# Eight sets of second-layer weight forms, at another place in the planner's order

## The chip, the cores and the metric

The kernel runs on one core of a Trainium2 chip. The metric is the device time of one execution in microseconds, as the median of several runs. A profile of one execution stands beside the times. Engines are named as the profile does: PE (TensorE matmul; PEld is its weight load), DVE (VectorE), ACT (ScalarE), POOL (GpSimd) and SP (SyncE, which issues most DMAs).

## The reference

Eight batch elements pass through an attention block and then an MLP-mixer block, all in float32:

```
x / rms(x) * g on q and k                # 12 heads, 448 positions, 64 wide
attn = softmax(q k^T / 8);  x = attn v   # -> x: 448 x 768 for each element
u  = x + (relu(x^T w_tok1) w_tok2)^T     # token mixing, 256 hidden
out = u + relu(u w_ch1) w_ch2            # channel mixing, 1536 hidden
```

## The kernel before, in words

**Elements and phases.** The elements are taken in turn. For element b the kernel emits token mixing (`tok1`, L833, and `tok2`, L876), the first channel layer (`ch1`, L987) and the second one (`plain_2`, L1041, for b = 1; `ch2`, L1055, from b = 2 on). The attention of element b+1 is merged in between as steps (`att_step`, L656; `big_step`, L587): scores into PSUM (L458), exponentials on ACT (L462), sums of them on DVE (L499), values (L531), and for the pair of heads after it the loads of q and k (L1375), squares on ACT (L1394), their sums on DVE (L1408), a Newton root (L1449 to L1451), the scaling (L420) and a transposition (L435). "Product (m, i)" below is `ch1`'s product i of hidden block m, m = 0 to 2, i = 0 to 6.

**Fewer products by sums of weights.** Both channel layers use schemes that trade products for sums of blocks, so that sums of the weights ("forms") have to be made first, on the chip.
- `sum_items` (L242) makes the first layer's: SP loads four blocks into a tile of the pool `raw` (L276), POOL makes four more (L249 to L252), SP stores them to DRAM (L256). `ch1` reads them through `load_units` (L915, DMA L927), up to seven weight units ahead.
- `form_items` (L291) makes the second layer's, in eight sets g = 0 to 7. A set takes three `raw` tiles a, b and c out of a pool of five. `load` issues four DMAs on SP (L304 twice, L305, L306) from the stored plain weights into a and b. Four `part`s then make 16 additions of 128x128 on POOL (L320), the last part also three copies (L324) and, on POOL's own DMA queue, two stores (L310, L311). Only `ch2` of element 2 and after needs them, and `load_units` reads none of them until all eight sets have been emitted.

**`ch1`'s seven products.** Each goes to a PSUM tile `m_ps` of two that alternate, and is drained: i = 0 and 4 by a copy on ACT (L1009, L1021), the others by an addition on DVE (L1005). After i = 4, POOL makes two additions (L1005) into `hb` and `r[2]`; DVE's addition of i = 5 reads that `r[2]`.

**What sets the order.** PE, DVE, ACT and POOL run in the order in which the program emits them. Items carry a cost, `run` (L166) adds the costs up on a planner's clock, and `later(us, fn)` (L158) emits a function when that clock has passed its due time. SP is not in the list of the hand-ordered engines (L88): its DMAs stand in nearly, but not exactly, the order of emission. `form_items` is called behind element 1's token mixing (L1240). Counted from that call, in the planner's units, and added up from the items' costs: product (0,4) is emitted at 29.8, (1,1) at 53.7, (1,2) at 58.8, (1,3) at 63.6, (1,4) at 67.0, (1,5) at 73.5, (2,1) at 88.6, (2,4) at 103.1, (2,5) at 108.4. The twelve halves of `plain_2` begin at 119.2 (the third is at 139.0, the fifth at 160.9, the eighth at 180.5). The second half of element 2's x leaves for DRAM at 187.0 (`send_x`, L780, DMA L786), is loaded back, turned, at 194.0 (`load_x`, L792, DMAs L795 and L798), and element 2's token mixing, which reads it at L837 and L844, begins at 204.2.

Of the kernel before, what the change touches and what calls it, by code (L numbers as in the profile page):

```python
# [83 lines left out]
def whole(ctx, tc, shifted, pre, q, k, v, g_q, g_k, moe_w_tok1, moe_w_tok2, moe_w_ch1, moe_w_ch2, out):  # L84
# [73 lines left out]
    def later(us, fn):  # L158

        at = clock[0] + us  # L160
        i = len(pending)
        while i and pending[i - 1][0] > at:
            i -= 1
        pending.insert(i, (at, fn))
# [37 lines left out]
    def raw_tile():  # L202
        return raw_pool.tile([P, WCOLS, 2], U32, name="raw")
# [87 lines left out]
    def form_items():  # L291


        G, FORMS_FROM, FORMS_EVERY = range(8), 10.0, 20.0
        plain = lambda g: wp2[:].rearrange("p (m h x k t) n -> p x h t m k n", m=3, h=2, x=2, k=3)[
            :, g // 4, g // 2 % 2, g % 2]
        made = ws2[:].rearrange("p (f c) n -> p c f n", c=8)
        eight = lambda t: t[:].rearrange("p n w -> p (n w)").bitcast(F32).rearrange("p (q n) -> p q n", q=8)

        def load(g):  # L300
            a, b, c = st["form", g] = [eight(raw_tile()) for _ in range(3)]
            src = plain(g)
            for m in range(2):
                nc.sync.dma_start(out=a[:, 3 * m:3 * m + 3], in_=src[:, m])  # L304
            nc.sync.dma_start(out=a[:, 6:8], in_=src[:, 2, 0:2])  # L305
            nc.sync.dma_start(out=b[:, 7], in_=src[:, 2, 2])  # L306

        def send(g):
            a, b, c = st.pop(("form", g))
            nc.gpsimd.dma_start(out=made[:, g, 0:8], in_=c)  # L310
            nc.gpsimd.dma_start(out=made[:, g, 8:NF9], in_=b[:, 0:7])  # L311
            st["formed"] += 1

        def part(g, i):
            a, b, c = st["form", g]
            at = dict(d=a[:, 4], s=a[:, 6], v=a[:, 7], y=a[:, 3])
            at.update({(m, k): a[:, 3 * m + k] if 3 * m + k < 8 else b[:, 7] for m in range(3) for k in range(3)})
            at.update({f: c[:, f] if f < 8 else b[:, f - 8] for f in range(NF9)})
            for o, x, op, y in W_STEPS[4 * i:4 * i + 4]:
                nc.gpsimd.tensor_tensor(  # L320
                    out=at[o], in0=at[x], in1=at[y], op=ALU.add if op == "+" else ALU.subtract)
            if i == 3:
                for f, x in W_SINGLE:
                    nc.gpsimd.tensor_copy(out=at[f], in_=at[x])  # L324
                send(g)

        for g in G:
            at = FORMS_FROM + g * FORMS_EVERY
            later(at, lambda g=g: load(g))
            for i in range(4):  # L330
                later(at + 8.0 + 2.5 * i, lambda g=g, i=i: part(g, i))
# [890 lines left out]
    for b in range(B):  # L1222
        early, double = middle_items(b)
        if b == 0:
            early, last = first_items(
                tok1_items(0, 0) + x_items(0, 1) + tok1_items(0, 1) + early, double, some)
        else:
            if b > 1 and in_next(b - 1):

                y, z = sends(b - 1, y_order(b - 1)[:4]), left  # L1230
                left = [y[0], y[1], z[0], y[2], z[1], y[3]]
            run(merge(tok1_items(b, 0), left[:2]))
            begin, early = merge(tok1_items(b, 1) + early[:3 * KC], left[2:]), early[3 * KC:]
            if b == 1 and not shifted:
                run(merge(begin, sums[5:9]))
                early, begin = merge(early[:8], sums[9:]) + early[8:], []
            elif b == 1:
                early, begin = merge(begin + early[:8], sums[5:]) + early[8:], []
            if b == 1:
                form_items()  # L1240
            tail, keep = (4, 2) if b == 1 else (11, 6)
            last, ends = double[-tail - keep:-tail], double[-tail:]
            double = double[:-tail - keep]
            early = begin + early + double
# [33 lines left out]
class Start:  # L1278
# [67 lines left out]
    def plain(self, p):  # L1346

        return p < 2 * self.NPAIR
# [177 lines left out]
```

## Time and profile before

| | us |
|---|---|
| median of 3 runs | 1302.79 (1302.38 to 1304.1) |
| the profiled execution | 1300.44 |
| its span, first to last instruction | 1298.5 |
| mean granted PE clock | 0.993 |
| busy PE / DVE / ACT / POOL | 1250.2 / 793.8 / 392.3 / 383.4 |
| L320, 128 additions: first and last start | 300.5, 408.2 |
| L320, one: least / median / longest | 0.448 / 0.456 / 1.382 |
| L310 and L311, 8 each: one on POOL | 0.905 and 0.971 |
| landing of L310 / L311, median | 5.0 / 6.5 |
| landing of the loads L304 | 4.0 |

Lines of the timeline read: start, duration, engine, line, operation, output<-input, shape, count, and in brackets the idle time of the engine before it with what ended it. The table by windows gives, for each stretch of the span, its length, each engine's busy time with the number of instructions, the granted PE clock, the busy share of the DMA engines and what they moved in GB/s. A line of the waits is: who waited, for whom, us in total, how often, the longest.

### The profile page before, as it was taken

To read this page: it belongs to the slowest core of one execution; us is meant where nothing else is said; L and a number is where in the kernel's file an instruction comes from. 1 tells how busy PE (TensorE), PEld (TensorE's weight loads), DVE (VectorE), ACT (ScalarE), POOL (GpSimd) and SP (SyncE) were. 2 spreads that over 40 slices of the span, in tenths; PEclk is the share of its full clock that TensorE was granted. 3 is DMA by queue.
4 is the path that set the end of the run, shared out by engine and by line. 5 is a ranking of instruction groups with operands and counts; after the bars stand their busy time and mean duration, and the time that the engine had idled before them with its cause. 6 is when DMAs were issued, how large, how long until landed. Compare 5 with 4: busy or idle time off the path is not lost.

```text
span 1298.5 us, 20006 instructions
## 1 busy us (share of the span) xinstructions
PE 1250.2 (96%) x7228; PEld 889.8 (69%) x7228; DVE 793.8 (61%) x1229; ACT 392.3 (30%) x781; POOL 383.4 (30%) x641
## 2 busy tenths in 40 slices
PE   5998999997899999999999999999999999999996
PEld 3444444455654577895787868785887868797996
DVE  6988769754655256765658366765558456554233
ACT  5663433222322043312343034311343033300210
POOL 1303440047887012231132222231122322131231
PEclk9999999998999999999999999999999999999998
DMA  9667585997899567685766867595866964386553
GB/s 207 174 183 180 155 226 146 216 258 208 248 275 217 121 148 172 152 229 117 173 167 144 218 141 175 140 224 116 188 156 149 232 140 136 117 200 156 180 174 79
DMA packets 492864, 228.37 MB, mean 176 GB/s; under 512 B 375508, under 2 KB 453332, under 8 KB 492756
## 3 DMA queue, kind: packets, MB, share of 16 engines
q1 hardware_dynamic: 476178, 213.10, 66.6%
q0 software_dynamic: 3584, 12.06, 3.0%
q10 hardware_dynamic: 12994, 1.84, 0.8%
q8 instruction: 59, 0.97, 0.3%
q14 instruction: 49, 0.40, 0.1%
HBM read 184.26 MB, written 42.66 MB: 175 GB/s over the span
## 4 chain that ended last, share of the span: by engine, by line
PE 84%; DVE 6%; DMA 3%; POOL 2%; issue 2%; ACT 1%; SPq 1%; ACTq 0%; DVEq 0%; POOLq 0%
PE m_ps L999 23%; PE m_ps L1065 21%; PE s_ps L458 9%; PE o_ps L531 9%; PE m_ps L879 5%; PE m_ps L969 5%; PE m_ps L1048 4%; PE t_ps L837 2%; PE m_ps L837 2%; DMA ws<-raw 1%; PE m_ps L511 1%; PE d_ps L511 1%; POOL raw L320 1%; PE t_ps L432 1%; DVE raw L348 1%
## 5 line engine op out<-in xcount | busy, mean ns | idle before, releaser
L1065 PE MATMUL m_ps<-hb,unit 128*128 128x224 f32 x1440 | 277.2, 354 | 0.0
L1065 PEld LDWEIGHTS m_ps<-hb,unit 128*128 128x128 f32 x1440 | 271.0, 190 | 8.8 <-issue 7.7
L999 PE MATMUL m_ps<-tu,unit 128*128 128x224 f32 x1008 | 201.6, 355 | 1.3 <-ACT r L1009 1.3
L999 PEld LDWEIGHTS m_ps<-tu,unit 128*128 128x128 f32 x1008 | 189.1, 190 | 15.0 <-issue 9.9
L462 ACT ACTIVATE e<-s_ps 128x448 f32<-128x448 f32 x294 | 138.3, 549 | 174.6 <-PE s_ps L458 166.2
L999 PE MATMUL m_ps<-uT,unit 128*128 128x224 f32 x756 | 153.6, 358 | 13.7 <-DVE hb L1005 11.5
L999 PEld LDWEIGHTS m_ps<-uT,unit 128*128 128x128 f32 x756 | 144.0, 192 | 21.6 <-DVE hb L1005 13.0
L458 PE MATMUL s_ps<-qkT 64*64 64x448 f32 x1260 | 144.6, 545 | 0.8 <-ACT x L819 0.8
L531 PE MATMUL o_ps<-e,v 64*64 64x448 f32 x1148 | 131.4, 538 | 0.3 <-ACT uT L568 0.2
L1005 DVE TENSOR_TENSOR hb<-m_ps,r 128x448 f32<-128x448 f32 x63 | 39.1, 621 | 120.5 <-POOL r L1005 68.9
L499 DVE TENSOR_TENSOR es<-es,e 128x896 f32<-128x896 f32 x90 | 103.2, 1146 | 14.4 <-ACT e L462 9.0
L1005 POOL TENSOR_TENSOR hb<-r,r 128x448 f32<-128x448 f32 x21 | 23.8, 1135 | 245.4 <-ACT r L1021 245.4
L458 PEld LDWEIGHTS s_ps<-qkT 64*64 64x64 f32 x1260 | 45.7, 132 | 69.6 <-issue 60.1
L531 PEld LDWEIGHTS o_ps<-e,v 64*64 64x64 f32 x1148 | 46.4, 133 | 63.1 <-issue 58.4
L1006 ACT ACTIVATE hb<-hb 128x448 f32<-128x448 f32 x84 | 48.4, 577 | 111.8 <-DVE hb L1005 76.6
L879 PE MATMUL m_ps<-w_sb,h 128*128 128x448 f32 x192 | 75.3, 544 | 3.3 <-DVE uT L884 3.3
L1438 POOL TENSOR_TENSOR nt<-rs 128x56 f32<-128x56 f32 (+1 forms) x57 | 19.5, 341 | 198.1 <-DVE rs L1430 195.1
L1080 POOL TENSOR_TENSOR uT<-uT,r 128x448 f32<-128x448 f32 x42 | 51.4, 1240 | 78.3 <-DVE r L1080 46.6
L320 POOL TENSOR_TENSOR raw<-raw 128x128 f32<-128x128 f32 x128 | 68.0, 551 | 16.1 <-DMA ws<-raw 5.9
L884 DVE TENSOR_TENSOR uT<-uT,m_ps 128x448 f32<-128x448 f32 x48 | 29.3, 613 | 63.0 <-PE m_ps L879 63.0
L1005 DVE TENSOR_TENSOR r<-m_ps,r 128x448 f32<-128x448 f32 x42 | 26.1, 622 | 64.7 <-PE m_ps L999 64.7
L1408 DVE TENSOR_REDUCE ms<-sq 128x28 f32<-128x896 f32 (+2 forms) x44 | 47.4, 1080 | 28.6 <-ACT sq L1394 25.0
(141 smaller groups left out, 1585.0 us busy)
## 6 DMA issues: line engine op xcount, KB each, us to landing
unit<-ws SPq DMA_DIRECT2D x267, 384.0 KB, 4.1
raw<-in_moe_w_ch_dram SPq DMA_DIRECT2D x72, 256.0 KB, 3.5
v<-in_v_dram SPq DMA_DIRECT2D x96, 112.0 KB, 3.9
xs<-xt SPq DMA_DIRECT2D x56, 168.0 KB, 4.4
out_dram<-turned SPq DMA_DIRECT2D x168, 56.0 KB, 2.0
qk_t<-in_q_dram SPq DMA_DIRECT2D x144, 56.0 KB, 3.7
qk_t<-in_k_dram SPq DMA_DIRECT2D x144, 56.0 KB, 3.6
x<-xs SPq DMA_DIRECT2D x42, 192.0 KB, 4.1
```

The lines of the kernel that those rows point to most:

```text
L320: nc.gpsimd.tensor_tensor(out=at[o], in0=at[x], in1=at[y], op=ALU.add if op == "+" else ALU.subtract)
L458: nc.tensor.matmul(out=pss[i][rows_of(i, a), 0:S], lhsT=qkT[h, 1, k * D:(k + 1) * D], rhs=qkT[h, 0, :], start=True, stop=True)
L462: nc.scalar.activation(out=e[:, i, :], in_=pss[i][:, 0:S], func=AF.Exp)
L499: nc.vector.tensor_tensor(out=es[:], in0=(es if k > 1 else st["e", t, 0])[:], in1=st["e", t, k][:], op=ALU.add)
L531: nc.tensor.matmul(out=st["o", p][a * D:(a + 1) * D, 0:S], lhsT=vt[rows, k * D:(k + 1) * D], rhs=e[rows, :], **kw)
L837: nc.tensor.matmul(out=st["t1", h][jc][:, 0:HC], lhsT=w1_sb[:, c, jc * P:(jc + 1) * P], rhs=st["x", b, h][:, :, c, :], start=start and c = ...
L879: nc.tensor.matmul(out=ps[:, 0:S], lhsT=st["h1", jc][:, cc * P:(cc + 1) * P], rhs=w2_sb[:, jc].rearrange("p c r -> p (c r)"), start=(jc == ...
L969: nc.tensor.matmul(out=ps, lhsT=a[:, o + 2 * half, :], rhs=natural(half * KF + t) if wide else u[:, half * KC + t, :], start=(t == 0 and h ...
L999: nc.tensor.matmul(out=ps[:, j * HS:(j + 1) * HS], lhsT=w[:, t, j, :], rhs=m, start=(t == 0), stop=(t == KC - 1))
L1005: add = lambda e, o, x, y: e.tensor_tensor(out=o, in0=x, in1=y, op=ALU.add)
L1048: nc.tensor.matmul(out=ps, lhsT=w[:, t, :], rhs=natural(half * KF + t), start=(half == 0 and t == 0), stop=(half == 1 and t == KF - 1))
L1065: nc.tensor.matmul(out=ps[:, x * HS:(x + 1) * HS], lhsT=st["w"][:, tile_at % 6, :], rhs=hb[:, X_SLOT[f], i, :], start=(i == 0), stop=(i == 3))
```

## The change

Two numbers in `form_items`. Set g was due at 10 + 20 g planner units after the call, its parts 8.0, 10.5, 13.0 and 15.5 later; now it is due at 55 + 18 g. The last part's due time goes from 165.5 to 196.5. Nothing else differs; all sets, operations and DMAs are the same.

```diff
     def form_items():
...
-        G, FORMS_FROM, FORMS_EVERY = range(8), 10.0, 20.0
+        G, FORMS_FROM, FORMS_EVERY = range(8), 55.0, 18.0
...
         for g in G:
             at = FORMS_FROM + g * FORMS_EVERY
             later(at, lambda g=g: load(g))
             for i in range(4):
                 later(at + 8.0 + 2.5 * i, lambda g=g, i=i: part(g, i))
```

## The prediction, on record

> **What bounds the kernel now.** I began with the table by windows, because the page has PE busy for 96% of the span: only the stretches where it is not can give anything.
>
> ```profile
> 276.00:320.00 44.00, 34.94 (x221) 24.54 (x220) 25.11 (x45) 12.47 (x27) 25.22 (x49) 0.88 0.79 225
> 320.00:360.00 40.00, 34.08 (x230) 24.35 (x228) 23.29 (x32) 14.03 (x30) 34.51 (x63) 1.00 0.89 250
> 360.00:400.00 40.00, 40.00 (x224) 22.36 (x224) 25.58 (x41) 13.90 (x29) 36.01 (x64) 1.00 1.02 254
> 400.00:437.00 37.00, 37.00 (x111) 18.46 (x104) 14.33 (x24) 3.71 (x8) 14.08 (x32) 1.00 0.94 225
> 437.00:586.00 149.00, 148.97 (x908) 115.29 (x907) 92.38 (x136) 45.28 (x92) 36.57 (x58) 1.00 0.66 160
> ```
>
> The first number after the length is PE's busy time. From 360 on, PE has no gap until the tail. In the two windows before, element 1's first channel layer, it lacks 9.06 + 5.92 us, and the granted clock falls to 0.88. As all behind is PE without a gap, a microsecond won here is won at the end. The timeline of PE shows where they lie:
>
> ```profile
> 293.62 4.81 PE L999 MATMUL m_ps<-tu,unit 128*128 128x224 f32 x24
> ...
> 303.80 2.54 PE L999 MATMUL m_ps<-tu,unit 128*128 128x224 f32 x12
> 315.39 7.05 PE L999 MATMUL m_ps<-uT,unit 128*128 128x224 f32 x24 [9.06 <-DVE hb L1005]
> ...
> 337.54 2.54 PE L999 MATMUL m_ps<-uT,unit 128*128 128x224 f32 x12 [2.16 <-ACT r L1021]
> ...
> 346.53 2.54 PE L999 MATMUL m_ps<-uT,unit 128*128 128x224 f32 x12 [1.01 <-DVE hb L1005]
> 350.52 2.54 PE L999 MATMUL m_ps<-uT,unit 128*128 128x224 f32 x12 [1.46 <-DVE hb L1005]
> 354.36 2.54 PE L999 MATMUL m_ps<-tu,unit 128*128 128x224 f32 x12 [1.29 <-ACT r L1009]
> ```
>
> So the waits are 9.06 and 2.16 + 1.01 + 1.46 + 1.29 = 5.92. The 24 products behind the long one take 7.05 where 24 took 4.81: another 2.24, the clock being at 0.50 from 312 to 320. Who holds DVE's L1005 is seen on POOL, and then on DVE:
>
> ```profile
> 300.50 3.84 POOL L320 TENSOR_TENSOR raw<-raw 128x128 f32<-128x128 f32 x8 [5.94 <-DMA ws<-raw]
> ...
> 306.06 3.70 POOL L320 TENSOR_TENSOR raw<-raw 128x128 f32<-128x128 f32 x8
> 309.70 0.77 POOL L324 COPY raw<-raw 128x128 f32<-128x128 f32 x3
> 310.53 0.92 POOL L310 DMA_DIRECT2D ws<-raw  x1
> 311.45 0.99 POOL L311 DMA_DIRECT2D ws<-raw  x1
> 312.45 1.14 POOL L1005 TENSOR_TENSOR hb<-r,r 128x448 f32<-128x448 f32 x1
> ```
>
> ```profile
> 314.71 0.62 DVE L1005 TENSOR_TENSOR hb<-m_ps,r 128x448 f32<-128x448 f32 x1 [15.56 <-POOL r L1005]
> ```
>
> POOL's two additions of product (0,4) had their input at 299.0 (ACT's copy L1021 ends there) and started at 312.45. Before them in POOL's order stand set 0's 16 additions, three copies and two stores, and these waited 5.94 us for a `raw` tile that the first layer's sums still held. DVE stood behind that, and PE behind DVE.
>
> The smaller waits come from SP. Its waits, and ACT's timeline:
>
> ```profile
> SPq L304 <- POOL raw L324: 12.4, 2, 11.0
> ```
>
> ```profile
> 333.85 0.95 ACT L1394 ACTIVATE sq<-qk_t 128x896 f32<-128x896 f32 x1 [8.07 <-DMA qk_t<-in_k_dram]
> ```
>
> Set 1's load stood on SP for 11.0 us until set 0 gave its tile back. The loads of q and k queued behind it; ACT waited 8.07 us for the last, and root, scaling and drains came late in a row.
>
> **The change, part by part.** Operations and DMAs are the same: 128 + 24 on POOL, 16 stores on POOL's queue, 32 loads on SP (about 2.1 us of SP's issuing a set, 386.96 to 389.4 for set 7). Only their place differs.
>
> *Set 0 leaves product (0,4).* No form stands before its additions; of the sums, one tile does (4 x 0.456, from 294.6 on), so they run from 299.0 to 301.3. DVE drains at once, and the `m_ps` tile that product (1,0) wants is free before PE comes to it at 306.34. Gain 9.06, and without a gap no slow clock: 2.24. Bounds: if the sums' tile came 5 us late the additions would end at 306.3, just in time, so I see no loss here. The Trainium skill, "TensorE: Matmul & The Clock Gate", part 1, has the clock halve after an idle window of some 3.4 us and need as long to return; by that the cost of the gap would be about half of 3.4, 1.7, beside the 2.24 of the row. I keep the row.
>
> *SP is no longer held.* Ahead of the q and k loads for the next pair go away: 11.0 (the wait), 3.4 (two waits of L306 for stores), and the issuing of sets 0, 1 and 2, three times some 1.95: 20.2 us. PE itself comes 9.06 + 2.24 = 11.3 earlier, so against PE the loads gain 8.9 us, where ACT lacked 8.07. That covers it, by less than a microsecond. In product row 0, where no form stood before (0,4), the same steps made no gap on PE. So I take the 5.92 as gone, with 0 as the other bound.
>
> *Sets 0 to 2 come to rows 1 and 2.* Set 0 is loaded between (1,1) and (1,2). On the new time axis, 17.2 earlier than the old one from (2,3) on, that is about 311; it lands some 4.4 later, and parts 0 and 1 (8 x 0.47 = 3.8, or 6.1 at set 3's pace, whose 16 took 12.27) end by 319.3 to 321.7. The additions of (1,4) have their input at 321.1, so they wait 0 to 0.6 us, and DVE asks for them only at 326.1. Behind (1,4), parts 2 and 3 follow and set 1, all done by some 342. Set 2's load (at 336) waits for tiles that set 0's stores free (330 + 6.5), lands at 341, and two parts stand before (2,4): until 347.2 at the slow pace, against an input at 348. What is then asked soonest is the hidden block at `plain_2`'s first half, for which the additions may end as late as 354.8, after 350.3. So the cover is some 5 us. The bounds are 0 and the 11.3 that the same queue cost in row 0; nearest are the 0.60 us that DVE waited for POOL in row 2 with set 4 before it. I take 1.0 for this row and the sharing beside it.
>
> The Trainium skill speaks against this place: "SBUF — State Buffer", section "SBUF: two separate sides", has GpSimd and a DVE operation with two SBUF inputs take one pair of ports in turn, each blocking the other for a whole instruction. The row agrees: 16 additions took 12.27 us beside DVE's L499 and L420, 7.5 alone. By the rule all three sets would be slow, which is the 1.0 again or up to 3 us more.
>
> *Sets 3 to 7 lie beside `plain_2`.* They need 10.2 to 15.1 us of POOL each (set 3 on: 15.1, 10.2, 11.1, 15.0, 11.8; set 2: 10.2; mean 12.2); 18 units there are 15.3 us (85 units in 72.3). POOL has nothing else but the 4 us of the root for pair 20. Set 7 would end at about 421, 438 on the old axis; POOL's next work, L903, starts at 450.84. Cover: 12 us.
>
> *Past the x path.* SP now issues sets 6 and 7 shortly before x's second half. There x leaves when DVE has turned it (420.87, so 403.7 new), its loads are issued by 431.15 and land at about 435.8, and PE reads it at 441.47: a cover of 5.7. Set 7's load needs the tiles of set 5, freed at 315.5 + 6 x 12.2 + 4.6 (two pairs of additions) + 6.5 = 400; with 2.1 of issuing it is past at 402. Cost nothing. DMA engines are 0.94 to 1.02 busy there, and their slowest landing on this path was 7.3 against 4.6: twice 2.7 still stays within 5.7.
>
> *Sum.* 9.06 + 2.24 + 5.92 - 1.0 = 16.2, from the profiled 1300.44: 1284.2. The median of the runs is 1.0018 times the profiled execution, so 1286.5.
>
> **The rivals.**
> 1. *Only the long wait goes.* If SP is busy otherwise (it issued without a pause from 315 to 331), the q and k loads stay late against PE, and the 5.92 stays: 1302.8 - 11.3 = 1291.5. For it: the cover of under a microsecond. Against it: row 0.
> 2. *The wait comes back at (2,4).* If set 2's load is held on SP by h, PE waits h - 5.3. With the 11.0 of the row that is 5.7, and the slow clock 2.24: 1294.4. For it: the tiles turn round in the same way, and 6.2 was seen once later (L304 for a store), which would cost 1. Against it: the sums are done by then and hold no tile.
> 3. *Slower: POOL falls behind and SP's queue carries it to x.* Each us more on a set's mean moves the tile for set 7's load by 6. Past 13.4 us a set (1.6 + 5.7 over 6, on 12.2) x's second half comes late. The gain is used up at 15.7, and the kernel is measurably slower from 16.2. At 17 PE waits 21.6 + 2.24: 1310. For it: two sets took 15, and DMA is full there. Against it: the mean is 12.2, no set took 16.
> 4. *No change.* The same wait is built again elsewhere, by SP's order, which the source does not fix: 1302.8.
>
> **How the numbers follow.** The forecast has 0.54 (1284 to 1289), rival 1 0.20, rival 2 0.12, rival 4 0.05, rival 3 0.09. The predicted time is the likeliest case's, 1286.5. The range takes in the forecast and rivals 1 and 2, from 1283.5 (nothing given back, and 2 us of PE's small issue gaps) to 1297; rivals 3 and 4, 0.14, are left out. A measurement here can tell about 0.2%, 2.6 us, from no change. Faster: 0.54 + 0.20 + 0.12 = 0.86; within: 0.05; slower: 0.09.
>
> **What would show it.** In the changed profile: no gap of PE before (1,0) and DVE's L1005 there not waiting for POOL; PEclk 1.00 throughout 276 to 320; ACT's square without the 8 us behind the load of k; POOL's L320 from about 315 to 420; SP's L304 without a wait of 11. It is wrong if PE shows a gap near (2,4), at the first half of `plain_2` or at L844 of element 2, or if L320 runs past 433.

## The result, and the profile after

| | before | after |
|---|---|---|
| median, same chip, us | 1303.44 (4 runs, 1302.38 to 1304.88) | 1288.87 (4 runs, 1285.49 to 1290.48) |
| profiled execution, us | 1300.44 | 1290.15 |
| its span, us | 1298.5 | 1288.2 |
| its mean PE clock | 0.993 | 0.994 |

The ratio is 0.9886, with a 95% interval of 0.9871 to 0.9901. By the medians the kernel is 14.6 us faster, where 16.2 were forecast.

The table by windows of after, for the stretches shown of before, with the last ones cut finer (length, busy time of PE, PEld, DVE, ACT and POOL with instructions, PE clock, DMA share, GB/s):

```profile
276.00:320.00 44.00, 43.72 (x283) 30.55 (x282) 30.11 (x55) 16.93 (x35) 15.98 (x26) 1.00 0.99 258
320.00:360.00 40.00, 38.41 (x251) 28.21 (x250) 28.26 (x43) 14.19 (x31) 35.21 (x61) 1.00 0.85 236
360.00:400.00 40.00, 40.00 (x189) 18.13 (x188) 26.28 (x40) 10.94 (x23) 37.32 (x70) 1.00 0.89 218
400.00:420.00 20.00, 20.00 (x55) 10.12 (x54) 6.50 (x12) 1.89 (x5) 8.92 (x26) 1.00 1.14 282
420.00:437.00 17.00, 14.80 (x41) 7.54 (x40) 1.27 (x2) 1.36 (x3) 13.45 (x29) 0.90 0.97 253
```

In the first two windows PE lacks 0.28 + 1.59 us instead of 9.06 + 5.92, and the clock is 1.00. A new lack of 2.20 stands in the last window, with the clock at 0.90. The timeline of PE in after shows each of them:

```profile
309.35 4.70 PE L999 MATMUL m_ps<-uT,unit 128*128 128x224 f32 x24
...
337.30 2.54 PE L999 MATMUL m_ps<-uT,unit 128*128 128x224 f32 x12 [0.29 <-DVE hb L1005]
341.14 2.54 PE L999 MATMUL m_ps<-tu,unit 128*128 128x224 f32 x12 [1.30 <-ACT r L1009]
...
431.37 1.07 PE L844 MATMUL t_ps<-x,w_sb 64*128 64x384 f32 x4 [2.20 <-DMA x<-xs]
432.37 5.83 PE L837 MATMUL t_ps<-x,w_sb 128*128 128x384 f32 x12
```

The same place in the timeline of PE before, where nothing waits:

```profile
442.22 0.81 PE L844 MATMUL t_ps<-x,w_sb 64*128 64x384 f32 x4
442.96 4.14 PE L837 MATMUL t_ps<-x,w_sb 128*128 128x384 f32 x12
```

Product (1,0), the 24 matmuls at 309.35, follows without a wait and takes 4.70 us, not 7.05. Of the four later waits 0.29 and 1.30 are left. New is the wait at L844, element 2's token mixing, for the second half of x. The groups behind it run at a slow clock: 1.07 and 5.83 us, not 0.81 and 4.14. So this place costs 2.20 + 0.26 + 1.69 = 4.15 us.

How far PE is ahead of before, from the starts and durations of equal instructions in the two profiled executions:

| point | before | after | ahead, us |
|---|---|---|---|
| start of product (1,0) | 315.39 | 309.35 | 6.04 |
| its end | 322.44 | 314.05 | 8.39 |
| end of the last product that waits (354.36 and 341.14, + 2.54) | 356.90 | 343.68 | 13.22 |
| end of L837 behind L844 | 447.10 | 438.20 | 8.90 |
| end of the span | 1298.5 | 1288.2 | 10.3 |

The first step is 6.04 and not 9.06 because this profiled execution of after had lost 3 us earlier, where nothing of the change is emitted. In element 0's token mixing PE waits 2.76 us at 112.79 before and 2.77 us at 112.76 after, for the same DVE instruction. Behind it the clock differs. The window from 112 to 118 in before, and then in after (the clock stands third from the end):

```profile
112.00:118.00 6.00, 5.21 (x32) 2.95 (x36) 5.90 (x10) 2.25 (x4) 2.95 (x5) 1.00 0.83 244
```

```profile
112.00:118.00 6.00, 5.24 (x16) 3.49 (x17) 5.90 (x10) 0.99 (x2) 2.73 (x5) 0.51 0.81 245
```

The half clock put PE's next pieces 2.97 us later (9.06 - 2.97 = 6.09, and 6.04 is seen). Without it this pair would differ by some 13.3 us, and the medians differ by 14.6. Among the profiles of this study the window has the clock at 1.00 in six, at 0.72 in two and at 0.51 or 0.52 in two, whatever the kernel. So an execution wins or loses up to 3 us there that the change does not touch. That this also makes the spread of after's runs (1285.49 to 1290.48) is likely, not shown.

On the other engines, POOL in after:

```profile
302.25 1.24 POOL L1005 TENSOR_TENSOR hb<-r,r 128x448 f32<-128x448 f32 x1 [0.70 <-ACT r L1021]
...
323.07 3.90 POOL L320 TENSOR_TENSOR raw<-raw 128x128 f32<-128x128 f32 x8 [16.71 <-DMA raw<-wp]
326.92 1.14 POOL L1005 TENSOR_TENSOR hb<-r,r 128x448 f32<-128x448 f32 x1
```

The additions of (0,4) wait 0.70 us for ACT, their input, and for nothing else. Set 0 begins at 323.07, not at 315, since SP issued its load only from 317.25 on (the line stands below), and so the additions of (1,4) start at 326.92, 2.6 us behind the end of ACT's copy (324.35). Nothing waits for them: DVE comes to the addition that reads them at 332.52, and they end at 329.15. In row 2 the additions of (2,4) start 2.0 us behind their input (354.20 against 352.20), behind half of set 2; DVE waits 2.50 us for them, where it waited 0.60 before, and PE still starts `plain_2` without a gap. And ACT's square behind the loads of q and k, which had waited 8.07 us:

```profile
319.22 0.95 ACT L1394 ACTIVATE sq<-qk_t 128x896 f32<-128x896 f32 x1 [1.83 <-DMA qk_t<-in_k_dram]
```

SP's queue in after, set 0's load first and then the way to L844 (start, then the time that the issues took):

```profile
317.25 0.96 SPq L304 DMA_DIRECT2D raw<-wp  x2
...
403.35 1.01 SPq L304 DMA_DIRECT2D raw<-wp  x2
...
405.58 2.65 SPq L408 DMA_DIRECT2D v<-in_v_dram  x4
...
409.96 0.90 SPq L304 DMA_DIRECT2D raw<-wp  x2
...
413.31 6.25 SPq L786 DMA_DIRECT2D xs<-xt  x4
...
423.79 2.70 SPq L798 DMA_DIRECT2D x<-xs  x2
```

DVE had turned the second half of x at 407.63:

```profile
406.99 0.64 DVE L824 STREAM_TRANSPOSE xt<-uT 128x448 f32<-128x448 f32 x1
```

SP sent it only from 413.31 on, 5.7 us later, because sets 6 (403.35) and 7 (409.96) and the loads of v stand ahead of it in SP's order. In before, SP sent at 420.87, at once. The sends then took 6.25 us (4.33 before), and the two loads of L798 took 2.70 (1.24 before).

### The profile page after: what moved, and what is told of

The parts are those of the page before. It is cut to its first block, busy times and chain, and to the rows that moved or that the text cites. A ratio compares the mean times of both kernels' runs of the same rounds, so it can differ in the third digit from the quotient of the medians.

```text
span 1288.2 us, 20010 instructions
## 1 busy us (share of the span) xinstructions
PE 1251.4 (97%) x7228; PEld 890.5 (69%) x7228; DVE 794.4 (62%) x1229; ACT 392.2 (30%) x781; POOL 381.7 (30%) x641
## 4 chain that ended last, share of the span: by engine, by line
PE 84%; DVE 7%; DMA 3%; SPq 2%; issue 1%; ACT 1%; POOL 0%; DVEq 0%; ACTq 0%; POOLq 0%
PE m_ps L999 25%; PE m_ps L1065 21%; PE s_ps L458 9%; PE o_ps L531 9%; PE m_ps L879 5%; PE m_ps L969 5%; PE t_ps L837 2%; PE m_ps L837 2%; PE m_ps L1048 1%; PE m_ps L511 1%; PE d_ps L511 1%; DMA x<-xs 1%; PE t_ps L432 1%; DVE es L499 1%; DVE raw L348 1%
## 5 line engine op out<-in xcount | busy, mean ns | idle before, releaser
L499 DVE TENSOR_TENSOR es<-es,e 128x896 f32<-128x896 f32 x90 | 102.8, 1142 | 14.6 <-ACT e L462 9.3
```

What stands on the lines that cost most here:

```text
L499: nc.vector.tensor_tensor(out=es[:], in0=(es if k > 1 else st["e", t, 0])[:], in1=st["e", t, k][:], op=ALU.add)
```

## The experiments

The first four ran on one chip, beside 15 runs of the kernel before with a median of 1303.62 us; the last four on another, beside 17 runs with 1304.68. Ratios are to these; those on record differ from the quotients of the medians by up to 0.0016 (experiment 4: 0.9906 against 0.9922), some 2 us, and smaller effects should not be read from either alone.

**1. Is it only POOL's order?** The kernel before, with the two additions behind (0,4) on DVE, so that set 0 can't hold them.

```diff
-            add(nc.gpsimd, h["B22"], r[5], r[3])
-            add(nc.gpsimd, r[2], r[2], r[5])
+            e = nc.vector if (b, mp) == (1, 0) else nc.gpsimd
+            add(e, h["B22"], r[5], r[3])
+            add(e, r[2], r[2], r[5])
```

> The kernel before, with one edit: the two additions after product (0,4) of element 1 are made by DVE in place of POOL, so nothing waits for POOL's queue there; the forms stay where they were. My theory (two separate causes: POOL's order, and SP standing on set 1's load): PE's wait of 9.06 us before product (1,0) goes, but SP still stands 10 to 11 us on L304, the q and k loads land at about 333 as before while PE comes some 11 us earlier, so ACT's square waits 15 to 19 us in place of 8.07, PE's later waits grow from 5.9 to 12 to 17 us, and the time falls by 0 to 5 us only. Rival (POOL's order alone made the time): PE's later waits stay near 5.9 and the time falls by the full 11.3 us, to about 1292.

Measured: 1303.84 us (10 runs), ratio 0.9999 (0.9988 to 1.0011). Nothing is won, though the wait of 9.06 is gone. PE's timeline, and then SP's waits (total, how often, longest):

```profile
324.69 2.21 PE L531 MATMUL o_ps<-e,v 64*64 64x448 f32 x4 [10.87 <-DMA v<-in_v_dram]
```

```profile
SPq L304 <- POOL raw L324: 12.1, 2, 10.5
```

SP stands on set 1's load for 10.5 us, and with it the loads of v and of q and k behind it; PE now waits 10.87 us for v (I had expected it to wait for q and k). The two waits of before, POOL's and SP's, ran side by side. One hid the other, and each alone is enough to stop PE. The rival that it was only POOL's order (1292) falls.

**2. The same pace, begun 20 units later, not 45.**

```diff
-        G, FORMS_FROM, FORMS_EVERY = range(8), 10.0, 20.0
+        G, FORMS_FROM, FORMS_EVERY = range(8), 30.0, 20.0
```

> The kernel before with the sets due at 30 + 20 g: behind product (0,4), but among the last of the first layer's sums. My theory: the 9.06 and the 2.24 of slow clock go; SP stands at most 5 us on L304 in this stretch, so of the 5.92 at least half goes too: 13 to 17 us faster, 1287 to 1291; x's second half is as early as in the kernel before, since set 7's load comes before its sends, so PE's wait at L844 of element 2 is under 0.5. Rival (the first layer's sums, which hold raw tiles, are what SP waits for, so only leaving them altogether helps): SP stands 8 us or more and the 5.92 stays, 1292 or more.

Measured: 1290.83 us (4 runs), 0.9886 (0.9871 to 0.9901). The long wait goes, but later waits of 2.44 + 1.26 + 1.46 + 1.29 = 6.45 us stay; I had expected half of the 5.92 to go. SP is hardly held here: its longest pause from 302 to 324 is 1.1 us, ahead of set 1's load. But the forms' loads stand among those of q and k, as its timeline shows, and then ACT's:

```profile
317.30 0.92 SPq L304 DMA_DIRECT2D raw<-wp  x2
...
319.31 3.87 SPq L1375 DMA_DIRECT2D qk_t<-in_k_dram  x4
```

```profile
325.73 0.95 ACT L1394 ACTIVATE sq<-qk_t 128x896 f32<-128x896 f32 x1 [8.58 <-DMA qk_t<-in_k_dram]
```

SP is through with k at 323.18, in after at 316.68. So the issuing of sets 0 and 1 ahead of these loads is enough for the small waits, without a long hold. No wait at L844 is seen.

**3. The change, with set 7 alone held back** behind the sends and loads of x.

```diff
-            at = FORMS_FROM + g * FORMS_EVERY
+            at = FORMS_FROM + g * FORMS_EVERY if g < 7 else 196.0
```

> The changed kernel with set 7 alone due at 196 in place of 181, behind the loads of x's second half. My theory (x's second half is late because SP has sets 6 and 7 to issue ahead of its sends): the sends leave about 2 us earlier, PE's wait at L844 (2.20) and the slow clock behind it (1.95) go or fall below 1 together; set 7's additions run beside token mixing until about 443, with no wait on PE; 2 to 4 us faster than the changed kernel. Rival (the DMA engines' load makes the transfers slow, whatever SP's order): x's sends and loads take as long, the wait at L844 stays at 1.5 or more.

Measured: 1284.49 us (5 runs), 0.9842 (0.9828 to 0.9855): faster than both kernels, 4.4 us under the change by the medians (0.9842 against 0.9886, with intervals that do not touch). SP's timeline:

```profile
409.42 7.26 SPq L786 DMA_DIRECT2D xs<-xt  x4
```

The sends start 3.9 us earlier and the wait at L844 is gone, though the sends take no less than in after (7.26 and 6.25 us): so it is SP's order that made this wait, and not the slow transfers alone. The only PE wait of size left from 276 to 445 is the 1.29 at L1009. Set 7's additions end at 438, and L903 follows on POOL at 440.98 without harm.

**4. The change at a quicker pace,** 15 units a set.

```diff
-        G, FORMS_FROM, FORMS_EVERY = range(8), 55.0, 18.0
+        G, FORMS_FROM, FORMS_EVERY = range(8), 55.0, 15.0
```

> The changed kernel with the sets due at 55 + 15 g, so that set 7 is loaded at 160, ahead of x's sends. My theory: PE's wait at L844 goes or falls below 1, as set 7's load is off SP before x's second half is ready; set 2 now has all four parts before the additions of (2,4), which end some 5 us later, for a PE wait of 0 to 3 us at the start of plain_2; together 1284 to 1289. Rival (DMA load): the transfers are packed closer, the wait at L844 stays at 1.5 or more.

Measured: 1293.46 us (4 runs), 0.9906 (0.9889 to 0.9923). The waits of PE, and one of SP's:

```profile
363.21 4.78 PE L1048 MATMUL m_ps<-hb,unit 128*128 128x448 f32 x12 [2.44 <-DVE hb L1005]
...
436.29 1.82 PE L844 MATMUL t_ps<-x,w_sb 64*128 64x384 f32 x4 [2.38 <-DMA x<-xs]
```

```profile
SPq L304 <- DMA ws<-raw: 24.8, 4, 10.5
```

The wait behind (2,4) comes, as expected. SP held set 2's load for 10.5 us, as rival 2 has it, but POOL did not wait for that load: it went from set 1 to set 2 without a pause (350.10 and 350.12), and all 16 additions stood ahead of those of (2,4). So this is POOL's order again, as in row 0. The wait at L844 does not go, as I had thought it would. The sets are due closer together than POOL makes them, so SP stands on tiles that POOL's stores have yet to free (24.8 us in all; 11.7 in after), which is rival 3's path at a small size. Set 7's load is past SP at 408.84, before x is turned (412.37), but a hold of 4.0 us ahead of set 6's load (390.51) had put back all behind it, four loads of v took 5.17 us (2.65 in after), and x goes out at 416.85. The rival's sign, a wait of 1.5 or more, came as well: this run does not tell SP's queue from the crowded transfers.

**5. Set 0 alone left in its old place,** the others spread as in the change.

```diff
-            at = FORMS_FROM + g * FORMS_EVERY
+            at = 10.0 if g == 0 else 55.0 + 18.0 * (g - 1)
```

> The kernel before, but only set 0 stays at 10; sets 1 to 7 come at 55 + 18 (g - 1). This frees SP of set 1 to 3's loads ahead of the q, k and v loads, and leaves set 0 in front of POOL's additions of (0,4). My theory (two causes side by side, either of which alone holds PE about 11 us): PE's 9.06 before (1,0) and the slow clock stay, nearly the same size; the 5.9 of later waits falls to 1.3 to 2; 4 to 6 us faster than before, 1297 to 1300. Rival (SP's queue is the only cause): PE's wait before (1,0) falls below 3 and the time to 1290 or less.

Measured: 1297.49 us (10 runs), 0.9955 (0.9939 to 0.9971). SP is freed of the holds at L304, POOL's order is as before, and PE's timeline has the long wait again:

```profile
317.67 7.68 PE L999 MATMUL m_ps<-uT,unit 128*128 128x224 f32 x24 [10.16 <-DVE hb L1005]
```

Of the later waits 0.15 + 1.29 are left. So with the long wait in place the early loads of the sets behind set 0 make 4.5 of the 5.92, by way of SP, and moving them is worth 0.45% by itself.

**6. The edits of 1 and 5 together.**

> The last kernel with, as in the first experiment, the two additions after (0,4) made by DVE, so that both causes are away though set 0 still stands early. My theory: no wait of PE over 1.5 us between 276 and 360; with set 7 loaded at 163 x's second half is in time; 16 to 20 us faster than before, 1284 to 1288. Taken one at a time the two edits give about 0 and 4 to 6, so together far more than their sum. Rival (the forms have to leave the stretch for another reason, such as the ports they share with DVE): waits of 4 us or more stay there, 1290 or more.

Measured: 1290.53 us (6 runs), 0.9905 (0.9883 to 0.9926). Edit 1 alone gave 0.0% and edit 5 alone 0.45%, together they give 0.95% (12.4 us; 14.2 by the medians): more than their sum, as two waits side by side should. But 1284 to 1288 had been expected, and 0.59 + 1.25 + 1.47 + 1.58 + 1.29 us of PE waits are left. SP's waits from 276 to 330 point to the cause:

```profile
SPq L256 <- POOL raw L252: 8.1, 3, 3.8
```

The first layer's sums (L249 to L252) stand behind set 0 on POOL, SP waits to store them, and q and k queue behind those stores; ACT's square waits 7.96 us for k. That is a third link that I had not seen: set 0 delays q and k even when SP does not stand on L304. No run takes this link away alone; in the change, where set 0 stands behind these sums, SP's wait there is 1.4 and ACT's square waits 1.83. The time falls on the rival's side (1290 or more, the forms in the way for another reason), though no single wait is 4 us.

**7. The change at a slower pace,** 20 units a set.

```diff
-        G, FORMS_FROM, FORMS_EVERY = range(8), 55.0, 18.0
+        G, FORMS_FROM, FORMS_EVERY = range(8), 55.0, 20.0
```

> The changed kernel with the sets due at 55 + 20 g: set 6 at 175, close ahead of x's second half (187), set 7 at 195, behind its loads (194). My theory: as with set 7 alone moved, PE's wait at L844 is gone or below 1, 1284 to 1286. Rival (what counts is the last set load ahead of x's sends, whichever it is): set 6's load now stands where set 7's stood, the wait at L844 is 1 to 3 again, 1287 to 1290.

Measured: 1285.77 us (5 runs), 0.9862 (0.984 to 0.9885). Set 7's load now comes behind x's, set 6's still ahead of it. The timeline of PE:

```profile
427.32 1.19 PE L844 MATMUL t_ps<-x,w_sb 64*128 64x384 f32 x4 [1.14 <-DMA x<-xs]
```

The wait is half of after's and the clock stays at 1.00 behind it. I had said under 1; a wait of 1 to 3 was the rival's sign, that the last set ahead of x counts, whichever it is. The time is the one that I had expected. The interval touches that of the change, so that 20 is better than 18 is likely, not shown.

**8. No forms at all.** Where the wait at L1009 comes from, and what the forms cost in all. The second layer then reads plain weights in the forms' place, so that its output is not the reference's.

```diff
-        for g in G:
+        st["formed"] = 8
+        for g in ():
...
-        return l + [(4, False, six(ws2, i)) for i in range(NF9 * 8 // 6)]
+        return l + [(4, False, six(wp2, i % (NC * NF // 6))) for i in range(NF9 * 8 // 6)]
```

> The changed kernel without the forms: no set is loaded, added or stored, and the second layer of elements 2 to 7 reads the plain weights in their place, as many and as large transfers. It shows what the forms still cost. My theory (they are hidden but for the waits that the profile names): PE's waits in element 1's first layer stay at 0 to 1.3 us, none at L844, 1283 to 1285, within 1.5 us of the kernel with set 7 moved. Rival (a spread cost through DMA load and shared ports that no wait shows): 1281 or less.

Measured: 1282.57 us (5 runs), 0.9839 (0.9817 to 0.9861). No PE wait for any of this is left between 276 and 445, the 1.29 at L1009 included, so that one comes from the forms too. Against this floor the forms cost 6.3 us in the change and 1.9 us in experiment 3, by the medians; by the ratios the latter (0.9842 against 0.9839) can't be told from nothing. A further cost spread over the span (the rival, 1281 or less) is not seen; the low end of the interval, 0.9817 of 1304.68 or 1280.8, just reaches it.

## Why the prediction was right, and where it was wrong

- **"Set 0 leaves product (0,4)": right.** The 9.06 and the 2.24 are gone, and POOL's additions wait for ACT alone (0.70).
- **"SP is no longer held": right in the mechanism.** The wait of 11.0 at L304 is gone from there, ACT's square waits 1.83 instead of 8.07, and 4.33 of the 5.92 go. But the loads gained 6.2 us against PE (8.07 - 1.83), not the 8.9 worked out, so the cover of "less than a microsecond" was not there: 0.29 + 1.30 are left. Rival 1, in which the 5.92 stays, is what experiment 2 shows when sets 0 and 1 load among q and k.
- **The sum hid how the two stand to each other.** I added 9.06 + 2.24 and 5.92 as if each could be had alone. Experiment 1 gets nothing for the first without the second, experiment 5 gets 0.45% for the second without the first, and experiment 6 gets 0.95% for both. The sum holds only because one move removes both. Rival 1's 1291.5 stands for both gone and the small waits left; that is about what experiments 2 and 6 gave (1290.83, 1290.53).
- **"Sets 0 to 2 come to rows 1 and 2", 1.0: near enough.** Set 0 started 8 us later than worked out (323 for 315), since SP came to its load at 317.25 and not at 311: it had issued almost without a pause from 299.6 on what stood ahead. The additions of (1,4) were 2.6 us late where at most 0.6 was allowed, which DVE's own order covered, and those of (2,4) 2.0, which the cover of 5 us at `plain_2` took. PE shows no wait at either. The additions of sets 0 to 2 took 10.8, 9.1 and 9.3 us where set 1 had taken 7.5 before: all three are slow, as the prediction had feared of the ports, and no wait of PE came of it. The 1.30 at L1009 is of the forms' making (experiment 8).
- **"Sets 3 to 7 lie beside `plain_2`": right in the cost, late in the place.** They took 10.1 to 13.7 us of POOL each. Set 7 ended at 434, not 421, because POOL stood 10.19 us for set 6's load; L903 came at 441.95, so the cover held.
- **"Past the x path … Cost nothing": this step failed.** It had set 7's load past SP at 402, ahead of x at 403.7. The load was issued from 409.96 to 411.98, behind the turned x (407.63). As with set 0, its place in SP's order was left out: I had placed it by the time at which its `raw` tiles come free. In that order it stands behind set 6's load, which itself went out only at 403.35: before it SP had issued without a pause the sends of x's first half, q and k, and x's loads (384.69 to 402.4). The sends left 5.7 us late, and from there to the last load of x SP took 13.2 us where it had taken 10.3. The cover was 6.4 and not 5.7, because the matmuls at 441.47 still read the first half of x and those at 442.22 are the first to read the second. 5.7 + 2.9 - 6.4 = 2.2: PE waited 2.20, and the half clock made it 4.15. Experiment 3 takes set 7 away from there and wins 4.4 us. So the prediction's time came out near the truth partly by luck: the 4.15 that it missed, and the 1.59 for its 1.0, are offset in the medians by something over 3 us that the waits do not account for. In the profiled pair, 1.4 us of it are won in small pieces behind 438 (8.90 to 10.3 in the table above); the rest is within the executions' spread.
- **Rival 3**, "slower: POOL falls behind and SP's queue carries it to x", had the right path. POOL kept up, though, so that the queue alone did it, at 4.15 us and not 21.6 + 2.24. **Rival 2** did not come in the change. In experiment 4 PE waited 2.44 behind (2,4), but through POOL's order and not through the held load.
- What would make it wrong was named rightly: a gap at L844 of element 2 was on the list.

Left open: which of the crowded DMA transfers made the sends of x slower (6.25 us, and 7.26 in experiment 3, against 4.33). The DMA share is 1.14 from 400 to 420. A larger pool of `raw` tiles was not tried.

## What to carry to other kernels

Two waits that run side by side hide each other: take both away before you judge either, and look for who else queues behind each instruction that waits. A moved load must be placed in the issuing queue's order, behind all that goes out before it, and not at the time at which its buffers come free. When background work is spread out, its last piece is the one to check against the next deadline: holding back one set of eight was worth 4.4 us here.

## What the runs showed of the hardware

A short gap of PE does not always halve the clock. Behind the wait of 2.8 to 2.9 us at 112.8 the clock was 1.00, 0.72 or 0.51 over six us, in equal code. Behind 2.20 us (L844, after) and 2.38 us (L844, experiment 4) it halved for some 4 us. Behind 2.16 us (before, 337.54) and 2.44 us (experiment 2) the next 12 products took 2.54 us, as at full clock; behind 2.44 us in experiment 4 (363.21) the clock was 1.00 too. A halving cost some 1.7 to 3 us each time, behind these short gaps about as much as the gap.

The Trainium skill, "TensorE: Matmul & The Clock Gate", part 1, "What's actually happening", gives the clock a free-running window of about 3.4 us, which would make the same gap fall differently from run to run; the toss at 112 agrees with that. It also asks for at least one idle window before the clock halves, and here single waits of 2.20 to 2.91 us were followed by the half clock, so the measurement decides: a wait shorter than that is not safe.

SP's issuing is a resource of its own. A set's four loads take some 2.0 us of it where nothing holds them, four loads of q or k 1.9 to 4.5, four sends of x 4.3 to 7.3. In after, what stood ahead of x's sends added its whole time, though SP's longest wait there (402 to 414) was 0.5 us.
